# Ten transposes of r on TensorE instead of a DMA, w2 laid out by row block, score tails on ScalarE alone: an attention, MLP and soft-MoE chain on one core

## The chip, the cores and the metric

The kernel runs on one core of one Trainium2 chip. The metric is the device time of one execution in microseconds (us); the median of three runs is quoted. Engines are named as in the profile: PE (TensorE), DVE (VectorE), ACT (ScalarE), POOL (GpSimd) and SP, which here only issues DMAs. Instructions of one engine run in the order in which they stand, and wait for each other across engines by semaphores.

## The reference

Three layers follow each other. Attention has 4 batches, 8 heads, 576 positions and head size 64, with a threshold on the scores (only scores within `tau` of the row's maximum keep their weight). An MLP with a leaky ReLU follows, 512 to 2048 to 512. Last comes a soft mixture of 8 experts with 4 slots each, F = 1024.

```python
scores = scale * q @ k.T
thresh = max(scores, -1) - tau
scores = where(scores >= thresh, scores, -1e9)
attn = softmax(scores);  x = attn @ v            # x: 2304 x 512
h = x @ w_in;  g = maximum(0.01 * h, h);  x = g @ w_out
logits = x @ phi                                 # 2304 x 32
d = softmax(logits, axis=0);  slot_in = d.T @ x  # 32 x 512
for e in range(8):
    slot_out[e] = maximum(slot_in[e] @ w1[e], 0) @ w2[e]
out = softmax(logits, axis=1) @ slot_out
```

`w_in` and `w_out` come as 64-bit numbers and are turned into 32-bit ones on the chip by integer operations. `w1` and `w2` are 32-bit, 16.8 MB each.

## The kernel before

**Start (to about 135 us).** All 16 pieces of `w_in` (128 rows by 512 columns) are read as integer pairs into buffers `r`, converted by ACT, DVE and sometimes POOL (`one_chunk`, lines 606 to 680, by one of three recipes called modes 0, 1, 2; `MI` names the recipe of each of four rows), and split into a high and a low f16 part (`wh`, 8 buffers). The same is done to `w_out` (`MO`); its 32-bit form is also stored to a scratch tensor `scr`, and folded with `phi` into `wq`. The first attention tiles run beside this.

**Attention.** There are 18 tiles of 128 rows, each with four head pairs. `ends` computes the scores of the last 64 keys for all eight heads and keeps them in SBUF as `T` and their maxima in `tn`. For a head pair, `heads` computes 2 x 512 scores into PSUM (`S`, two buffers, line 1089), DVE reduces their maxima (line 1098) and forms the threshold `th` (line 1103). ACT writes the thresholded main part from `S` (two instructions of 128x512, line 1112). The tail, 2 x 64 scores, is made in two steps: POOL or DVE adds the threshold to `T` (line 1121), then ACT applies its Prelu to the sum (line 1130). An exponential follows on ACT (line 1201), then a high and low f16 split, a DMA transpose (line 1235, `aT`), and the product with `v` into `X` (line 1259).

**Feed.** For a finished tile `xT`, four chunks of 512 columns go through 12 matmuls each (line 1340, into PSUM `h` or `eT`), ACT's leaky ReLU (`g`, line 1352) and an f16 split `r` (lines 1359 to 1366). `r` is used twice: untransposed by the slot sums `M` (line 1534), and transposed, as `rT`, by the logits `L` (lines 1385 and 1389). Each of the 72 chunks is transposed by one DMA (line 1375), issued by SP. After every second tile, `block` rescales the running sums.

**Experts, after the last tile.** From the slot sums a chain of small steps leads through `w_out` (line 1650, from `scr`) to the slot inputs. They meet `w1` (line 1702) and `w2` (line 1776). `w1` and `w2` are read in 512 KB pieces into any free buffer of the tags `wh`, `qk`, `r`, `ae`, `ah`, `e2`, some halves of `w1` (256 KB, `HF` of them in pairs) into smaller tags. A buffer is free when attention or the feed no longer uses it: `qk` after the last scores, `wh` after the last feed matmuls, `r` after the last slot sum. `w2` is read as three column parts (256, 128 and 128 columns). For one part a group of matmuls needs the pieces of four experts; after a part its columns are combined, multiplied with the routing weights and written out (line 1829).

**What sets the order.** A planner in the program (`Plan.schedule`) goes through all operations with an estimated cost and a priority each, simulates the engines, and fixes both the order on every engine and the buffer that each operation gets. The table `O` holds the priorities and sizes. A new number or cost there moves many instructions. The lines of the functions that the change touches:

## Time and profile before

| | |
|---|---|
| median of 3 runs | 621.42 us (618.77 to 626.65) |
| profiled execution, its time | 618.97 us |
| span of that execution, first to last instruction | 616.8 us |
| granted TensorE clock, mean | 0.930 of full speed |
| PE busy | 541.8 us, 88% |
| DVE busy | 425.1 us, 69% |
| ACT busy | 399.5 us, 65% |
| POOL busy | 257.5 us, 42% |

Busy shares are means over the three stages, which are limited by different things. They have to be read by stretches of time. Busy time counts an instruction from its start to its end, and on ACT and DVE the next one may start before that end, so the distance of two starts is the better measure of what one instruction takes from its engine.

### The profile page before, as it was taken

What the parts mean: (1) busy time and instruction counts of PE and PEld (TensorE: products, weight loads), DVE (VectorE), ACT (ScalarE), POOL (GpSimd) and SP (SyncE); (2) the same over time, 40 slices, a digit from 0 to 9 for tenths busy, and PEclk for the clock granted to TensorE, in tenths of its full rate; (3) what the DMA queues carried; (4) which work ended last, traced back from release to release, by engine and by line L of the source; (5) the groups of instructions that cost most, each with busy time, mean ns of one, the idle gap of its engine ahead of it and who ended that gap; (6) DMA issues with size and microseconds to landing.
All of it is one profiled execution on the core that took longest, in us unless ns stands there. A gap on an engine that the chain in (4) does not pass through costs nothing.

```text
span 616.8 us, 14389 instructions
## 1 busy us (share of the span) xinstructions
PE 541.8 (88%) x5576; PEld 313.0 (51%) x5576; DVE 425.1 (69%) x930; ACT 399.5 (65%) x720; POOL 257.5 (42%) x302
## 2 busy tenths in 40 slices
PE   4787787688999999999979999999999979589884
PEld 2465575454555555555445555556555555333463
DVE  3879989996879859688787788778776555320031
ACT  3977787585777878778957877786787823221031
POOL 0243264514346545555544667573666630120000
PEclk9999667799999999999979999999999989868997
DMA  8997676654999979999989889999999999999998
GB/s 314 398 249 196 233 192 209 159 150 92 208 216 203 177 137 176 163 253 168 200 138 164 163 157 196 224 166 201 150 167 205 141 204 241 261 415 368 413 414 332
DMA packets 254388, 135.93 MB, mean 220 GB/s; under 512 B 231152, under 2 KB 231664, under 8 KB 254320
## 3 DMA queue, kind: packets, MB, share of 16 engines
q1 hardware_dynamic: 248416, 118.85, 83.6%
q10 hardware_dynamic: 5904, 16.16, 8.8%
q8 instruction: 44, 0.72, 0.5%
q14 instruction: 24, 0.20, 0.1%
HBM read 69.44 MB, written 8.91 MB: 127 GB/s over the span
## 4 chain that ended last, share of the span: by engine, by line
PE 57%; DMA 15%; DVE 13%; ACT 9%; issue 3%; POOL 1%; SPq 1%; ACTq 0%; DVEq 0%; POOLq 0%
PE h L1340 14%; PE eT L1340 10%; PE S L1089 8%; PE X L1259 7%; DMA aT<-ah 5%; PE S L1702 2%; PE S L1057 2%; PE misc L1534 2%; DMA scr<-w 2%; PE misc L858 2%; ACT ae L1112 2%; DMA qk<-in_w2q 2%; DVE nm L1098 2%; DMA wh<-in_w 2%; DMA r<-in_w2q 2%
## 5 line engine op out<-in xcount | busy, mean ns | idle before, releaser
L1222 POOL TENSOR_TENSOR ah<-ae,ah 128x512 f16<-128x512 f32 (+1 forms) x192 | 185.7, 995 | 135.8 <-DVE ah L1211 55.4
L1340 PEld LDWEIGHTS <-xT 128*128 128x128 f16 x864 | 77.8, 98 | 87.7 <-issue 12.9
L1340 PE MATMUL h<-wh,xT 128*128 128x512 f16 x492 | 120.1, 383 | 0.5 <-ACT w L848 0.2
L1112 ACT ACTIVATE ae<-S,th 128x512 f32<-128x512 f32 x144 | 93.3, 684 | 26.2 <-DVE th L1103 12.1
L1098 DVE TENSOR_REDUCE nm<-S 128x2 f32<-128x1024 f32 x72 | 86.8, 1216 | 23.1 <-PE S L1089 22.6
L1259 PEld LDWEIGHTS <-aT 128*128 128x128 f16 (+1 forms) x2016 | 75.3, 103 | 44.0 <-issue 26.1
L1089 PE MATMUL S<-qk 64*128 64x512 f32 (+1 forms) x320 | 88.1, 688 | 9.2 <-DMA qk<-in_qk 5.6
L1340 PE MATMUL eT<-wh,xT 128*128 128x512 f16 x372 | 89.7, 379 | 0.0
L1259 PE MATMUL X<-vx,aT 128*128 128x65 f16 (+1 forms) x1792 | 74.1, 199 | 9.8 <-DVE x L1295 6.2
L1201 ACT ACTIVATE ae<-ae,c 128x1152 f32<-128x1152 f32 x64 | 80.3, 1255 | 1.3
L1366 DVE TENSOR_TENSOR r<-g,r 128x512 f16<-128x512 f32 x56 | 45.2, 807 | 3.3 <-ACT r L1361 2.9
L1352 ACT ACTIVATE g<-h,c 128x512 f32<-128x512 f32 x41 | 27.9, 681 | 22.0 <-PE h L1340 20.3
L1211 DVE CAST ah<-ae 128x1152 f16<-128x1152 f32 x52 | 40.3, 775 | 2.5 <-DMA aT<-ah 1.4
L1089 PEld LDWEIGHTS S<-qk 64*128 64x128 f32 (+1 forms) x320 | 23.2, 188 | 33.1 <-ACT ae L1112 9.9
L1359 DVE CAST r<-g 128x512 f16<-128x512 f32 x37 | 20.6, 555 | 23.6 <-ACT g L1352 21.8
L858 PE MATMUL misc<-c,w 128*128 128x32 f32 x128 | 24.7, 348 | 13.7 <-ACT w L848 8.3
L1366 POOL TENSOR_TENSOR r<-g,r 128x512 f16<-128x512 f32 x16 | 20.1, 1260 | 37.5 <-DVE r L1359 27.3
L1352 ACT ACTIVATE g<-eT,c 128x512 f32<-128x512 f32 x31 | 21.1, 681 | 19.6 <-PE eT L1340 16.7
L858 PEld LDWEIGHTS misc<-c,w 128*128 128x128 f32 x128 | 22.8, 267 | 19.3 <-ACT w L848 12.2
L663 POOL TENSOR_TENSOR w<-w,qk 128x512 int32<-128x512 int32 x8 | 11.5, 1434 | 40.3 <-DVE w L646 21.5
L1103 DVE SCALAR_TENSOR_TENSOR th<-nm,c,tn 128x2 f32<-128x2 f32 x72 | 26.2, 372 | 0.5
L1057 PE MATMUL S<-qk 64*128 64x64 f32 (+1 forms) x320 | 22.7, 289 | 1.9 <-DMA qk<-in_qk 0.9
(287 smaller groups left out, 924.2 us busy)
## 6 DMA issues: line engine op xcount, KB each, us to landing
r<-in_w_in SPq DMA_DIRECT2D x16, 512.0 KB, 4.5
qk<-in_w_out SPq DMA_DIRECT2D x14, 512.0 KB, 4.9
wh<-in_w SPq DMA_DIRECT2D x11, 512.0 KB, 7.6
qk<-in_qk SPq DMA_DIRECT2D x9, 576.0 KB, 4.2
qk<-in_w SPq DMA_DIRECT2D x10, 512.0 KB, 7.4
qk<-in_qk ACTq DMA_DIRECT2D x7, 576.0 KB, 5.5
scr<-w SPq DMA_DIRECT2D x14, 256.0 KB, 3.5
vr<-in_v ACTq DMA_DIRECT2D x10, 330.0 KB, 3.9
```

The lines of the kernel that those rows point to most:

```text
L858: pe.matmul(out=wpp.ap, lhsT=wt.ap[:, k], rhs=phi.ap[:, k], start=(k == 0), stop=(k == 3))
L1057: pe.matmul(out=Tp.ap[r0:r1, i, pr * KT : pr * KT + KT], lhsT=qk[b, pr].ap[h, 0, o : o + r1 - r0], rhs=qk[b, pr].ap[h, 1, KW:S], start=(pr ...
L1089: pe.matmul(out=ps.ap[r0:r1, i], lhsT=qk[b, pr].ap[h, 0, o : o + r1 - r0], rhs=qk[b, pr].ap[h, 1, 0:KW], start=True, stop=True, skip_group ...
L1098: lambda: dve.tensor_reduce(out=nm.ap, in_=ps.ap, axis=AX.X, op=ALU.max, negate=True),
L1112: (lambda i: lambda: act.activation(out=main()[:, i], in_=ps.ap[:, i], func=AF.Prelu, bias=th.ap[:, i : i + 1], scale=1.0, alpha=2.0**90))(i),
L1201: lambda: act.activation(out=ae.ap, in_=ae.ap, func=AF.Exp, bias=nt.ap[:, 0:1], scale=0.125),
L1211: ("dve", P2(t_dve2(2 * S)), lambda: dve.tensor_copy(out=ah.ap[:, :, :S], in_=ae.ap)),
L1222: lambda: pool.tensor_tensor(out=ah.ap[:, h, w0 : w0 + c1 - c0], in0=ae.ap[:, h, c0:c1], in1=ah.ap[:, h, c0:c1], op=ALU.subtract),
L1259: pe.matmul(out=xa(2 * pr + i)[r0:r1], lhsT=w()[:, r0:r1], rhs=vtiles[b, pr].ap[:, wv, cv, 0 : D + 1], start=(n == 0 and 2 * pr + i in (0, ...
L1340: pe.matmul(out=hp.ap, lhsT=xT.ap[:, wx * 4 + k], rhs=wh(k, j, ww), start=(n == 0), stop=(n == 11),)
L1352: (lambda g, hp, j: lambda: act.activation(out=g.ap, in_=hp.ap, func=AF.Prelu, alpha=0.01, scale=hsc.ap[:, j : j + 1]))(g, hp, j),
L1366: fg = lambda eng, j, g: lambda: eng.tensor_tensor(out=r[j](1), in0=g.ap, in1=r[j](0), op=ALU.subtract)
```

## The change

**r on TensorE.** For chunks 62 to 71 of 72 (`RT=62`; the last two of tile 15 and all of tiles 16 and 17) the DMA transpose is gone. PE transposes the 32-bit `g` in four blocks into a PSUM bank that belonged to `S`, ACT copies the high part into `rT`, and DVE subtracts to get the low part. These banks can be used only after the last scores.

**w2 by row block.** A 512 KB piece of `w2` now holds the same row block for four experts, so each piece is followed by its own 8 matmuls. Before, a group of matmuls waited for four pieces. The bytes and the size of a piece stay.

**Score tails.** The addition of the threshold by POOL or DVE is gone. ACT makes the tail from `T` in two instructions of 128x64 with the threshold as bias.

**Table.** `MI` is (0, 1, 1, 1) where it was (2, 0, 0, 1): 12 of 16 pieces of `w_in` go by recipe 1 and none by recipe 2. `HF` is 8, not 9 (pairs of half pieces of `w1`); `E` has one buffer, not two; buffers named `w` are not taken by others until `w_in` is converted. Some costs and priorities differ, so the planner draws the order anew.

```diff
-        NP=1, HB=1, HF=9, LH=2.09, ... E=2, ... MI=(2, 0, 0, 1), ... TE=0.12, ... NA=23, ... PJ=0,
+        NP=1, HB=1, RT=62, TB=1, HF=8, LH=2.27, ... E=1, ... MI=(0, 1, 1, 1), ... TE=0.21, ... NA=22, ... PJ=0.02,
...
+    pl.main["w"] = ("w", "w_in")
...
         tail = lambda: two(ae.ap[:, 2 * KW :]) if flat else ae.ap[:, :, KW:S]
+        if O["TB"]:
+            for i in range(2):
+                act_op(
+                    prio - 0.01, 230,
+                    (lambda i: lambda: act.activation(
+                        out=tail()[:, i], in_=Ts.ap[:, 2 * pr + i], func=AF.Prelu, bias=th.ap[:, i : i + 1],
+                        scale=1.0, alpha=2.0**90))(i),
+                    r=[Ts, th], w=[(ae, 2 + i)],
+                )
+            return
...
+            if 4 * t + j >= O["RT"]:
+                tp = bank([P, 4, P])
+
+                def f(g=g, tp=tp):
+                    for c in range(4):
+                        pe.transpose(tp.ap[:, c], g.ap[:, c * P : (c + 1) * P], ident.ap)
+
+                pe_op(p + 0.05, 530, f, r=[g, ident], w=[tp, rT[j]], work=427)
+                act_op(
+                    p + 0.05, t_act(512), (lambda j, tp: lambda: act.activation(
+                        out=rT[j].ap[:, 0:4], in_=tp.ap, func=AF.Copy))(j, tp), r=[tp], w=[(rT[j], 0)],
+                )
+                dve_op(
+                    p + 0.05, 608, (lambda j, tp: lambda: dve.tensor_tensor(
+                        out=rT[j].ap[:, 4:8], in0=tp.ap, in1=rT[j].ap[:, 0:4], op=ALU.subtract))(j, tp),
+                    r=[tp, (rT[j], 0), wq], w=[(rT[j], 1)],
+                )
+                continue
             dma_t(
...
-            if hf:
-                groups = [[load(a["w2q"][hf - 1, 4 * G + j], T0 - 7 + 0.1 * hf, [P, 8, QC]) for j in range(4)]]
-            else:
-                groups = [
-                    [load(a["w2"][4 * G + j, n], T0 - 7, [P, 4, HC]) for j in range(4)] for n in range(2)
-                ]
+            m = wd // QC
+            for x in range(4 * m):
+                w = load(
+                    a["w2q"][hf - 1, G, x] if hf else a["w2"][G, x], T0 - 7 + 0.1 * hf, [P, 4, 1024 // wd // 4, wd]
+                )
+                nc_ = 2 // m
...
-                    r=[(hts[G], (j, m)) for j in range(4) for m in ([n] if hf == 0 else [0, 1])] + ws
+                    r=[(hts[G], (j, nc_ * x // 4)) for j in range(4)] + [w]
```

The order moves at three places that matter below. Line numbers in the new order are those of the changed file, some 3 to 41 higher.

The first is SP's queue from the last transposes of attention (`aT`) and of r (`rT`) to the first pieces of `w1` (`in_w`) that go into `wh`, the feed's weight buffers. Before:

```order
L1375 DMA_TRANSPOSE rT<-r 128x8x128 x4
L1682 DMA qk<-in_w 128x1024
L1682 DMA x_7878<-in_w 128x512
L1682 DMA qk<-in_w 128x1024
L1682 DMA ah<-in_w 128x1024
L1375 DMA_TRANSPOSE rT<-r 128x8x128 x3
L1682 DMA ah<-in_w 128x1024
L1682 DMA wh<-in_w 128x1024 x2
L1375 DMA_TRANSPOSE rT<-r 128x8x128 x4
L1682 DMA rT<-in_w 128x512
L1682 DMA wh<-in_w 128x1024 x2
```

With the change:

```order
L1249 DMA_TRANSPOSE aT<-ah 128x9x128 x4
L1416 DMA_TRANSPOSE rT<-r 128x8x128
L1714 DMA qk<-in_w 128x1024 x2
L1649 DMA vx<-scr 128x512
L1714 DMA qk<-in_w 128x1024
L1649 DMA vx<-scr 128x512
L1714 DMA ah<-in_w 128x1024 x2
L1714 DMA x_7931<-in_w 128x512
L1714 DMA wh<-in_w 128x1024 x4
L1714 DMA r<-in_w 128x1024 x2
L1714 DMA wh<-in_w 128x1024 x2
```

No transpose stands between or behind the pieces of `w1` any more, and two pieces of `scr` have come to SP.

The second is ACT at the last chunks of the feed, from the rescaling of the block before (`dh`) to the last `g`, the leaky ReLU. Before:

```order
L1352 ACTIVATE g<-h,c_1354 128x512
L1513 ACTIVATE dh<-misc,c_4566 128x64
L1352 ACTIVATE g<-eT,c_1354 128x512
L1361 ACTIVATE r<-g 128x512
L1352 ACTIVATE g<-h,c_1354 128x512
L1420 ACTIVATE c_2064,c_2065<-lg,sm 128x32
L1352 ACTIVATE g<-eT,c_1354 128x512
L1420 ACTIVATE c_2064,c_2065<-lg,sm 128x32
```

With the change (`rT<-S` is the copy of a transposed chunk out of PSUM):

```order
L1554 ACTIVATE dh<-misc,c_5282 128x64
L1405 ACTIVATE rT<-S_77 128x512
L1375 ACTIVATE g<-h,c_1335 128x512
L1461 ACTIVATE c_2129,c_2130<-lg,sm 128x32
L1405 ACTIVATE rT<-S_77 128x512
L1375 ACTIVATE g<-eT,c_1335 128x512
L1405 ACTIVATE rT<-S_76 128x512
L1375 ACTIVATE g<-h,c_1335 128x512
L1405 ACTIVATE rT<-S_76 128x512
L1461 ACTIVATE c_2129,c_2130<-lg,sm 128x32
```

A copy of a chunk has come in behind each `g`, and the last copy follows the last `g` directly.

The third is ACT at a late head pair: main part, tail, feed, exponential. Before:

```order
L1112 ACTIVATE ae<-S_77,th 128x512 x2
L1130 ACTIVATE ae<-ae 128x2x64
L1201 ACTIVATE ae<-ae,c_116 128x1152
L1361 ACTIVATE r<-g 128x512 x2
L1352 ACTIVATE g<-h,c_1354 128x512
```

With the change:

```order
L1116 ACTIVATE ae<-S_77,th 128x512 x2
L1126 ACTIVATE ae<-T,th 128x64 x2
L1375 ACTIVATE g<-h,c_1335 128x512
L1215 ACTIVATE ae<-ae,c_116 128x1152
L1322 ACTIVATE xT<-h 128x512
```

Two instructions make the tail where one finished it, and they read `T` and `th` instead of a sum made elsewhere.

## Rows read from the trace of the kernel before

**Rows 1.** The page's slices: busy tenths in 40 equal slices of the span.
```profile
PE   4787787688999999999979999999999979589884
```

**Rows 2.** Two stretches: busy per engine (count), granted clock, DMA share, GB/s.
```profile
45.00:135.00 90.00, 68.42 (x517) 49.20 (x517) 85.70 (x190) 66.64 (x131) 37.91 (x34) 0.75 0.67 190
180.00:480.00 300.00, 293.83 (x3329) 162.24 (x3328) 235.72 (x484) 230.74 (x394) 174.73 (x196) 0.99 0.99 179
```

**Rows 3.** Groups by line and form, w_in's conversion: count, busy us, mean ns, idle before.
```profile
L638 DVE TENSOR_SCALAR w<-rT 128x512 int32<-128x512 int32 x17 | 9.0, 546 | 3.0 <-DMA scr<-w 2.7 <-ACT rT L611 0.2
...
L670 DVE SCALAR_TENSOR_TENSOR w<-rT,w 128x512 int32<-128x512 int32 x11 | 8.0, 726 | 0.0
...
L663 POOL TENSOR_TENSOR w<-w,r 128x512 int32<-128x512 int32 x4 | 5.5, 1370 | 11.9 <-DVE w L646 11.9
...
L622 ACT ACTIVATE r<-r,c 128x512 int32<-128x512 uint32 x4 | 3.1, 784 | 1.8 <-DMA r<-in_w_in 1.8
```

**Rows 4.** Groups by line and form, the score tails: count, busy us, mean ns.
```profile
L1130 ACT ACTIVATE ae<-ae 128x128 f32<-128x128 f32 x72 | 22.4, 311 | 1.9 <-DVE ae L1121 1.7
...
L1121 DVE TENSOR_TENSOR ae<-T,th 128x128 f32<-128x128 f32 x52 | 19.0, 366 | 4.1 <-POOL ah L1222 3.3 <-ACT T L1067 0.5
```

**Rows 5.** ACT in order of time: start us, us, instruction, idle before and its releaser.
```profile
483.88 0.31 ACT L1130 ACTIVATE ae<-ae 128x128 f32<-128x128 f32 x1
484.08 0.69 ACT L1352 ACTIVATE g<-h,c 128x512 f32<-128x512 f32 x1
...
485.83 0.32 ACT L1420 ACTIVATE c<-lg,sm 128x32 f32<-128x32 f32 x1
486.06 0.18 ACT L1420 ACTIVATION_READ_ACCUMULATOR c<-lg,sm 128x1 f32 x1
...
513.00 0.60 ACT L1308 ACTIVATE xT<-h 128x512 f16<-128x512 f32 x1 [0.98 <-PE h L1304]
```

**Rows 6.** PE in order of time, end of attention and of the feed.
```profile
496.35 0.93 PE L1259 MATMUL X<-vx,aT 128*128 128x65 f16 x14 [2.95 <-DVE x L1295]
...
512.36 0.60 PE L1304 MATMUL h<-c,x 128*128 128x128 f32 x4
512.80 1.46 PE L1340 MATMUL eT<-wh,xT 128*128 128x512 f16 x6
...
527.14 1.46 PE L1340 MATMUL eT<-wh,xT 128*128 128x512 f16 x6
...
535.30 0.23 PE L1385 MATMUL misc<-c,rT 128*128 128x64 f16 x1 [0.66 <-DMA rT<-r]
```

**Rows 7.** DVE in order of time: the split of a transposed tile.
```profile
513.63 0.69 DVE L1313 TENSOR_TENSOR xT<-h,xT 128x512 f16<-128x512 f32 x1 [0.42 <-ACT xT L1308]
```

**Rows 8.** SP's queue in order of time.
```profile
525.09 8.65 SPq L1375 DMA_TRANSPOSE rT<-r  x4
...
561.20 1.98 SPq L1682 DMA_DIRECT2D qk<-in_w  x3
```

**Rows 9.** Stretches of the end, columns as in Rows 2.
```profile
530.00:535.00 5.00, 1.26 (x24) 0.93 (x24) 0.57 (x1) 0.00 (x0) 0.00 (x0) 0.86 1.09 216
...
575.00:580.00 5.00, 5.00 (x84) 3.09 (x80) 0.84 (x8) 0.62 (x2) 0.00 (x0) 1.00 1.03 410
...
610.00:617.00 7.00, 0.89 (x5) 0.48 (x3) 1.29 (x2) 1.47 (x3) 0.00 (x0) 0.65 0.58 224
```

**Rows 10.** Chain that ended last, in order of time: start us, us, what.
```profile
526.84 8.41 DMA rT<-r x2
...
540.10 2.68 PE misc L1534 x24
...
557.67 10.36 PE S L1702 x80
...
593.55 11.10 DMA qk<-in_w2q
...
604.69 3.14 PE X L1776 x58
```

More of the change, by code (lines that the diff above doesn't have):

```diff
@@ L200, in place @@
             for tg in b.tag:
-                st = self.main.get(tg, tg)
-                if b.stream != st and b.stream not in self.early and pos.get(st, 0) < len(self.order.get(st, ())):
+                st = self.main.get(tg, (tg,))
+                if b.stream not in st and b.stream not in self.early and any(
+                    pos.get(x, 0) < len(self.order.get(x, ())) for x in st
+                ):
                     n, after = self.quota.get((b.stream, tg), (0, 0))
-                    if held[b.stream, tg] >= n or pos[st] < after:
+                    if held[b.stream, tg] >= n or pos[st[0]] < after:
                         continue
@@ L1062, in ends @@
         pe_op(
-            prio, 550, f, r=[qk[b, pr] for b in tile_parts(t) for pr in range(4)],
+            prio, 1040, f, r=[qk[b, pr] for b in tile_parts(t) for pr in range(4)],
             w=[Tp, tn, Ts], work=427,
@@ L1146, in f @@
                     pe.transpose(tp.ap[:, c - c0], ae.ap[:, c * P : (c + 1) * P], ident.ap)
-            pe_op(p2, 135 * n, f, r=[(ae, key), ident], w=[tp, (eT, key)], work=107 * n)
+            pe_op(p2, 135 * n, f, r=[(ae, k) for k in ((key,) if key < 2 else (2, 3))] + [ident], w=[tp, (eT, key)], work=107 * n)
             act_op(
@@ L1324, in emit, with bank @@
     HG = O["HG"]
+    banked = []
+    def bank(shape):
+        uniq[0] += 1
+        n = f"bk{uniq[0]}"
+        pl.early.add(n)
+        b = pl.buf(("B0", "B1", "B2", "B3"), shape, F32, n)
+        banked.append(b)
+        return b
     def feed(t, xT):
@@ L1598, in hbuf @@
         return pl.buf(("h", "eT"), shape, F32, f"hb{uniq[0]}")
-    def bank(shape):
-        uniq[0] += 1
-        n = f"bk{uniq[0]}"
-        pl.early.add(n)
-        b = pl.buf(("B0", "B1", "B2", "B3"), shape, F32, n)
-        banked.append(b)
-        return b
-    banked = []
     WO = T0 - 8
@@ L1862, in host @@
     w2 = np.asarray(inputs["moe2_w2"]).reshape(8, 2, P, 4, 4, P)
-    wa = w2[:, :, :, :, :2].reshape(8, 2, P, 4, 256)
-    wz = w2[:, :, :, :, 2:].transpose(4, 0, 2, 1, 3, 5).reshape(2, 8, P, 8, P)
+    w2 = w2.reshape(2, 4, 2, P, 4, 512).transpose(0, 2, 4, 3, 1, 5).reshape(2, 8, P, 4, 512)
+    wa = w2[..., :256]
+    wz = w2[..., 256:].reshape(2, 4, 2, P, 4, 2, P).transpose(5, 0, 1, 3, 4, 2, 6)
     def bits(w):
```

50 lines of the change are left out of this document (25 added, 25 removed).

## The prediction

> **What bounds the kernel now.** I read the slices of the page first [rows 1], then stretches of time, then the chain that ended last and the engines' own lists. Three stages show. Up to about 135 us PE is not full, because the converted weights are late: from 45 to 135 us DVE is busy 85.70 of 90 us, ACT 66.64 and PE 68.42, at a granted clock of 0.75 [rows 2]. From 180 to 480 us PE is the bound: 293.83 of 300 us at clock 0.99, with ACT at 230.74 and DVE at 235.72 [rows 2]. There at most 6.2 us can be had by any better order. The third stage is the end. The last feed matmuls start at 527.14 and end near 528.4, but the last logits start only at 535.30, released by the transposing DMA of r [rows 6]; the chain of waits books 8.41 us to that DMA [rows 10]. SP needs 8.65 us to issue the last four transposes [rows 8], and the reads of the expert weights stand behind them in that queue. Then a chain of small steps leads to `w1` at 557.67, and afterwards the reads set the pace: 410 GB/s with PE busy too [rows 9], while the chain books 11.10 us to the last awaited piece of `w2`, then 3.14 us to the matmuls behind it [rows 10]. What the change is worth is decided at the two ends, not in the middle.
>
> The profiled execution took 618.97 us (span 616.8, 2.2 around it). The median of the runs is 621.42, that is 2.45 above. The terms are summed against 618.97, and 2.45 is added for the median. I take 2% as what a measurement of this kernel can tell from no change: the three runs are spread over 1.3%.
>
> **Start.** By the two orders, up to the last write of the feed weights DVE loses 8 shifts (0.55 each by the mean) and gains 5 two-input integer steps (0.73 each), so 4.4 against 3.7 us [rows 3], and loses 8 tail additions of 0.37, 2.9 us [rows 4]. DVE gets 3.6 us less. POOL loses the four integer additions of 1.37 us on pieces of `w_in` [rows 3]. ACT has 8 more low-part steps in place of 4 cheaper ones, at most 8 x 0.78 = 6.3 us [rows 3], and dearer tails, below; its slack of 23 us in this stretch covers that if it falls well. DVE being 95% busy, I take 2.5 us of the 3.6 as time. Bounds: -5, if the POOL steps removed had also stretched DVE, and +2, if ACT becomes the late one. One buffer fewer for `E`, the guard on buffers `w`, and the shifted priorities I cost at nothing: the block steps have a whole tile pair between them. If that cover fails, a wait of one block step, below half a microsecond, comes up in each of 9 blocks; it lies within the bounds.
>
> **Score tails.** One ACT step of 128 columns takes 0.20 us from start to start (483.88 to 484.08), and one of 32 columns with a bias takes 0.23 (485.83 to 486.06) [rows 5]. Two tails of 64 columns with a bias are therefore between 0.40 and 0.52 us; I take 0.46. That is 0.26 more per head pair, 18.7 us of ACT over 72 pairs [rows 4]. In the middle stage some 15 us of it come on top of 230.74, ACT goes to 82%, and PE stays the bound [rows 2]. The cover is ACT's idle time; the exponential behind the tail is the one that is late if it fails. In return DVE loses 52 additions of 0.37 us [rows 4] and POOL the other 20, neither of them a bound there. Time: 0, with bounds -3 (half of PE's 6.2 us of idle time closes) and +18.7 (all of it shows).
>
> **r on TensorE.** The nearest rows are those of a tile `x`, which goes the same way. Four transposes take 0.44 us of PE (512.36 to the next matmul at 512.80) [rows 6], ACT's copy starts 0.64 after them and DVE's split 0.63 after that, ending at 514.32 [rows 5, 7]. From PE's start to a finished transposed chunk it is 1.96 us. PE thus gets 10 x 0.44 = 4.4 us of new work in a stretch that it fills; ACT gets 6 us and DVE 7, both half idle there. Against this, the last logits wait for about 0.8 us of leaky ReLU and 1.96 us, so they come 2.8 us after the last feed matmuls and not 6.9 us: -4.1. PE's wait of 2.95 us at 496.35 [rows 6] stood in the old order; I count half of it closed, -1.5, between nothing and all. The slot sums, which started 4.8 us behind the last logits (540.10) [rows 10], then come 7.6 us after the last feed matmuls and not 11.7. From 530 to 535 us the clock was still 0.86 [rows 9]; at the lower level the sums took 2.68 us [rows 10], at the higher one they would take half. I count half of that gain, -0.6. Together 4.4 - 4.1 - 1.5 - 0.6 = -1.8 us for the start of `w1`, with bounds +0.5 and -6.5 (the whole wait closed, and the clock held through `w_out` too).
>
> **The reads.** From 530 to 535 us the DMA engines moved 216 GB/s, 1.08 MB, which is nearly the four transposes of 0.262 MB alone [rows 9]: 1.25 us each, where plain reads at 410 GB/s need 0.64. Without them, and with the reads no longer behind them on SP, the `wh` pieces start as their buffers come free; about 7 us of reading come earlier. But the buffers are finite: the first `w2` pieces were issued at 561.20, 3.5 us after `w1` had started to give buffers back [rows 8, 10]. From there 30 pieces at 1.28 us are 38.4 us, and the last landed at 604.65, 43.45 us later; the other 5 us were backlog and a lower rate. With the change the gate opens 1.8 us earlier, 31 pieces are left and not 30 (+1.3, one pair of halves of `w1` fewer), and I count 3.5 us of the 5 us of backlog as gone, since the queue has caught up. Sum: -4.0 us for the last piece. Bounds: 0 (the gate decides and moves little) and -9 (the reads alone decide).
>
> [...]
>
> **The last step.** The last awaited group of 64 matmuls took 3.14 us after the last read [rows 10]; with eight per piece it is 0.4, so 2.7 less. After the reads the writes still move 224 GB/s of a possible 410 [rows 9], so part of the tail is transfer; I take -2, between 0 and -2.7. The pieces' size and the sum of their bytes do not move, so that layout itself costs nothing in reading.
>
> **Sum.** -2.5 + 0 - 4.0 - 2 = -8.5 us: 610.5 for an execution like the profiled one, **613** as the median, 1.4% below 621.42. Its own range, with the bounds of the single terms not all on one side, is 606 to 619.
>
> **Rivals.**
>
> First, the reads gain little: `w1` starts as late as before because PE's 4.4 us of transposes eat what the missing wait gives, and the pieces of `w2` wait for buffers as they did. For it speaks that PE fills the slices up to there [rows 1], so that its new work finds no hole; against it the 6.9 us of waiting before the logits. Only the start and the last step are left: -4.5, so 617. Chance 0.18.
>
> Second, all of it comes: start -4, the gate -6.5 with the clock held, the reads nearly -9, the last step -2.5, which gives about 603. For it speaks that the reads already run at 410 GB/s wherever they have buffers. Chance 0.20.
>
> Third, slower: ACT's two tails are the price. Every head pair needs ACT to clear `S` before PE may write the next scores. If ACT, at 82% or more and in order, comes late by its extra 0.26 us at each of 72 pairs, +18.7 us come on PE's path, less the gains of the end: 618.97 + 18.7 - 6.0 + 2.45 makes 634; with two thirds of it 628. It decides from the point where ACT's step in a pair, tails included, takes longer than PE's work per pair. Against it speaks that ACT has 69 idle us in 300. Chance 0.11 for 624 and more. [...]
>
> The forecast keeps 0.51. The **range 602 to 622** leaves out most of the third rival and the lower end of the second. Faster by over 2% means below 609.0: the second rival and about a quarter of the forecast, 0.32. Slower by over 2% means above 633.8: half of the third, 0.05. The rest is 0.63.
>
> **What would show it.** In the new profile no transpose of r stands on SP after the last one of attention. The last logits start within 3.5 us of the last feed matmuls. `w1` starts 14 to 18 us after that, and some 2 us earlier in the span than 557.67, apart from the shift of the start. The reads show no stretch of 216 GB/s near the end of the feed, and a short dip where the buffers are full. The matmuls behind the last piece of `w2` take under 1 us. PE is busy over 290 us between 180 and 480. If PE waits there for `ae`, the third rival is right; if the DMA rate falls well below 400 GB/s for over 6 us before the first pieces of `w2`, the gate decides and the first rival is right. The forecast is wrong if the feed begins later in the span than before, since everything behind it shifts.

## The result and the profile after

The changed kernel takes **604.86 us** (median of 4 runs, 602.83 to 617.41) against 620.96 for the kernel before in the same series. The ratio is 0.972, with a 95% interval of 0.967 to 0.978: 2.8% faster. One slow run of each kernel, 617.41 and 626.65 us, is left out of the ratio (the medians of the others, 603.44 and 620.51, lie 17.1 us apart), and the profiles of e1, e5 and e11 below are of slow runs too, so only waits within a stretch are read from them. The forecast was 613, 8.4 us below its median of 621.42; the gain is twice that, and the time lies near the lower end of the range. The profiled execution took 602.83 us, with a span of 601.0.

Where the 15.8 us between the two profiled executions lie is seen when the span is cut at four places on TensorE: the end of the last feed matmuls, the first slot-sum matmul of the last block, the first of `w1`, and the end. The right column is what the forecast's terms give for the stretch. Single differences can be 0.1 off by rounding.

| stretch, us | before | after | difference | forecast |
|---|---|---|---|---|
| up to the last feed matmuls | 528.6 | 520.8 | -7.8 | +0.4 (-2.5 + 0 + 4.4 - 1.5) |
| from there to the slot sums | 11.4 | 7.6 | -3.9 | -4.1 |
| from there to `w1` | 17.6 | 14.2 | -3.4 | -0.6 |
| from there to the end | 59.1 | 58.4 | -0.7 | -4.2 (-2.2 - 2) |

**The first stretch.** These are windows of the trace after: busy time of each engine with its count, then TensorE's granted clock, the DMA share and GB/s. The first two answer to [rows 2], the other three cut TensorE's full stage in parts.

```profile
45.00:135.00 90.00, 69.81 (x554) 48.83 (x553) 85.13 (x186) 74.93 (x148) 30.62 (x29) 0.75 0.70 203
180.00:480.00 300.00, 297.21 (x3424) 162.97 (x3422) 225.96 (x461) 244.22 (x454) 168.78 (x187) 1.00 1.02 181
...
215.00:330.00 115.00, 112.94 (x1228) 61.42 (x1225) 85.33 (x172) 95.65 (x179) 63.02 (x70) 1.00 1.03 182
330.00:480.00 150.00, 149.46 (x1762) 81.89 (x1758) 112.94 (x232) 117.84 (x220) 86.91 (x97) 1.00 1.02 180
480.00:520.83 40.83, 40.73 (x436) 24.46 (x428) 28.02 (x57) 20.22 (x39) 11.44 (x12) 1.00 0.96 244
```

The same three parts in the trace before, the last one up to its own last feed matmuls:

```profile
215.00:330.00 115.00, 110.43 (x1194) 61.60 (x1193) 89.82 (x204) 87.84 (x153) 62.01 (x70) 0.97 0.98 176
330.00:480.00 150.00, 148.44 (x1715) 80.99 (x1712) 114.61 (x223) 115.01 (x194) 88.58 (x98) 1.00 0.98 180
480.00:528.60 48.60, 44.17 (x491) 25.13 (x489) 25.22 (x58) 21.73 (x44) 15.37 (x16) 0.96 1.04 203
```

TensorE's idle time is the window less its busy time: 4.57 + 1.56 + 4.43 = 10.6 us before, 2.06 + 0.54 + 0.10 = 2.7 after. The clock adds to it: 0.97 over 110 busy us and 0.96 over 44 cost 3.3 + 1.8 = 5.1 us before and nothing after. Together that is 13.0 us less, minus the 4.4 us of new transposes (ten of 0.44, the distance from 518.93 to 519.37 below): -8.6, which is the whole of the first line of the table and 0.8 more. So nothing is left for the start: the first feed matmul does come earlier (110.68, not 114.92), but the 17th of the 144 leaky ReLUs on scores starts at 112.41 and started at 113.03.

**The wait for r.** TensorE in order of time in the trace after (start, duration, instruction, idle before it and its releaser):

```profile
518.93 0.60 PE L1401 MATMUL S<-c,g 128*128 128x128 f32 x4
519.37 1.46 PE L1363 MATMUL h<-wh,xT 128*128 128x512 f16 x6
521.67 0.66 PE L1401 MATMUL S<-c,g 128*128 128x128 f32 x4 [0.84 <-ACT g L1375]
523.74 0.19 PE L1430 MATMUL misc<-c,rT 128*128 128x32 f16 x1 [0.52 <-DVE rT L1409]
...
528.38 2.59 PE L1575 MATMUL misc<-r,dh 128*32 128x512 f16 x24
...
536.50 0.62 PE L1682 MATMUL eT<-raw,g 128*32 128x512 f32 x2 [0.75 <-ACT g L1674]
...
542.62 0.62 PE L1734 MATMUL S<-e,xT 128*32 128x512 f32 x1 [0.45 <-DVE xT L1702]
```

The last feed matmuls end at 520.8, the last logits start at 523.7, 2.9 us later where 2.8 was said and 6.9 stood before [rows 6]. One matmul of `w_out` takes 0.59 to 0.62 us here, at a clock of 1.00 (536.5 to 539.5 us); before it took 1.06 at 0.50 (549.2 to 552.7).

**The tails.** ScalarE in order of time, to be set beside [rows 5]:

```profile
479.02 0.60 ACT L1126 ACTIVATE ae<-T,th 128x64 f32<-128x64 f32 x2
479.50 0.70 ACT L1375 ACTIVATE g<-eT,c 128x512 f32<-128x512 f32 x1
```

Two tails take 0.48 us from start to the next start; 0.46 was the estimate from rows.

**The reads and the end.** Windows of the trace after, then SP's waits (total us, times, longest), then the end of the chain of waits (start, us, what), then the matmuls that wait for the last piece of `w2`:

```profile
535.00:540.00 5.00, 4.16 (x36) 1.36 (x36) 0.37 (x2) 0.60 (x1) 0.00 (x0) 1.00 0.61 220
...
555.00:560.00 5.00, 5.00 (x64) 2.28 (x58) 0.36 (x4) 1.09 (x2) 0.00 (x0) 1.00 1.03 410
```

```profile
SPq L1714 <- PE eT L1682: 6.4, 3, 5.7
...
SPq L1714 <- PE misc L1575: 5.1, 2, 4.7
```

```profile
542.62 8.79 PE S L1734 x80
552.43 4.24 PE S L1734 x37
556.67 10.53 DMA wh<-in_w
567.26 10.00 DMA r<-in_w2q
577.32 10.04 DMA qk<-in_w2q
587.43 6.51 DMA out<-wh
```

```profile
588.67 1.08 PE L1807 MATMUL X<-ah,ae 128*32 128x128 f32 x16 [0.62 <-DMA ah<-in_w2q]
```

Without the transposes the reads still fall to 220 GB/s for a while, because SP now waits for buffers that `w_out` and the slot sums give back. From 545 us on the DMA engines run without a pause, first with reads, then with writes, until 597: at 375 GB/s to 550 and at 409 to 421 from there. The chain ends in a write, no longer in the matmuls behind the last piece [rows 10].

### The profile page after: what moved, and what is told of

It reads as the page before. It is cut to its first block, busy times and chain, and to the rows that moved or that the text cites. A ratio compares the mean times of both kernels' runs of the same rounds, so it can differ in the third digit from the quotient of the medians.

```text
span 601.0 us, 14465 instructions
## 1 busy us (share of the span) xinstructions
PE 532.2 (89%) x5616; PEld 305.0 (51%) x5616; DVE 413.9 (69%) x890; ACT 417.3 (69%) x796; POOL 243.5 (41%) x282
## 4 chain that ended last, share of the span: by engine, by line
PE 32%; DMA 9%; issue 5%; DVE 5%; ACT 4%; POOL 2%; ACTq 0%; SPq 0%; DVEq 0%; POOLq 0%
PE h L1363 7%; PE eT L1363 7%; PE S L1093 5%; PE X L1273 4%; DMA aT<-ah 2%; PE S L1734 2%; DMA wh<-in_w 2%; DMA qk<-in_w2q 2%; DMA r<-in_w2q 2%; PE misc L1575 1%; ACT ae L1116 1%; POOL ah L1236 1%; PE S L1061 1%; DVE nm L1102 1%; DMA out<-wh 1%
## 5 line engine op out<-in xcount | busy, mean ns | idle before, releaser
L1363 PEld LDWEIGHTS <-xT 128*128 128x128 f16 x864 | 78.0, 98 | 88.9 <-issue 14.1
L1363 PE MATMUL h<-wh,xT 128*128 128x512 f16 x492 | 118.1, 379 | 1.4 <-ACT w L852 1.0
L1273 PEld LDWEIGHTS <-aT 128*128 128x128 f16 (+1 forms) x2016 | 73.3, 102 | 33.4 <-issue 22.8
L1273 PE MATMUL X<-vx,aT 128*128 128x65 f16 (+1 forms) x1792 | 71.7, 196 | 0.8 <-DMA aT<-ah 0.8
L1225 DVE CAST ah<-ae 128x1152 f16<-128x1152 f32 x53 | 42.1, 794 | 11.3 <-DMA aT<-ah 7.5
L1382 DVE CAST r<-g 128x512 f16<-128x512 f32 x47 | 25.7, 553 | 32.2 <-ACT g L1375 29.4
L1126 ACT ACTIVATE ae<-T,th 128x64 f32<-128x64 f32 x144 | 43.1, 351 | 0.0
L1093 PEld LDWEIGHTS S<-qk 64*128 64x128 f32 (+1 forms) x320 | 23.1, 188 | 36.9 <-ACT ae L1116 12.5
L1389 DVE TENSOR_TENSOR r<-g,r 128x512 f16<-128x512 f32 x51 | 37.6, 741 | 6.1 <-ACT r L1384 5.5
L1389 POOL TENSOR_TENSOR r<-g,r 128x512 f16<-128x512 f32 x21 | 24.9, 1190 | 39.5 <-DVE r L1382 32.7
L1375 ACT ACTIVATE g<-h,c 128x512 f32<-128x512 f32 x41 | 28.1, 685 | 16.0 <-PE h L1363 14.2
L1375 ACT ACTIVATE g<-eT,c 128x512 f32<-128x512 f32 x31 | 21.2, 683 | 18.8 <-PE eT L1363 16.1
L1107 DVE SCALAR_TENSOR_TENSOR th<-nm,c,tn 128x2 f32<-128x2 f32 x72 | 28.7, 406 | 0.3
L862 PE MATMUL misc<-c,w 128*128 128x32 f32 x128 | 21.8, 321 | 7.4 <-ACT w L852 4.4
L862 PEld LDWEIGHTS misc<-c,w 128*128 128x128 f32 x128 | 20.6, 243 | 13.6 <-ACT w L852 6.6
```

Of the source, the lines that this page charges most:

```text
L862: pe.matmul(out=wpp.ap, lhsT=wt.ap[:, k], rhs=phi.ap[:, k], start=(k == 0), stop=(k == 3))
L1093: pe.matmul(out=ps.ap[r0:r1, i], lhsT=qk[b, pr].ap[h, 0, o : o + r1 - r0], rhs=qk[b, pr].ap[h, 1, 0:KW], start=True, stop=True, skip_group ...
L1126: (lambda i: lambda: act.activation(out=tail()[:, i], in_=Ts.ap[:, 2 * pr + i], func=AF.Prelu, bias=th.ap[:, i : i + 1], scale=1.0, alpha= ...
L1225: ("dve", P2(t_dve2(2 * S)), lambda: dve.tensor_copy(out=ah.ap[:, :, :S], in_=ae.ap)),
L1273: pe.matmul(out=xa(2 * pr + i)[r0:r1], lhsT=w()[:, r0:r1], rhs=vtiles[b, pr].ap[:, wv, cv, 0 : D + 1], start=(n == 0 and 2 * pr + i in (0, ...
L1363: pe.matmul(out=hp.ap, lhsT=xT.ap[:, wx * 4 + k], rhs=wh(k, j, ww), start=(n == 0), stop=(n == 11),)
```

## The experiments

In e1 to e4, e8 and e11 to e15 the order on every engine stays the same as in the kernel that was edited, but for the instructions that the edit itself adds or takes away and a few steps of the last stage; in e9 and e10 it stays the same altogether. In e5 to e7 it is drawn anew by the same numbers. All ratios are to the kernel before, in the same series, with 95% intervals. These are the four stretches of the table above in the profiled executions of all runs but e5 and e6:

| us | last feed | to slot sums | to w1 | to the end |
|---|---|---|---|---|
| before / after | 528.6 / 520.8 | 11.4 / 7.6 | 17.6 / 14.2 | 59.1 / 58.4 |
| e1, e3 | 541.5, 537.5 | 7.4, 12.3 | 17.7, 13.1 | 57.9, 59.9 |
| e9, e13, e14 | 534.5, 531.3, 537.3 | 11.3, 10.2, 7.6 | 14.3, 14.4, 14.3 | 60.9, 60.5, 58.9 |
| e2, e4 | 524.0, 518.6 | 13.1, 8.0 | 17.5, 13.1 | 57.9, 59.8 |
| e7, e8, e10 | 527.0, 524.4, 535.6 | 7.5, 7.4, 7.4 | 17.7, 15.8, 16.2 | 58.2, 59.6, 58.5 |
| e11, e12, e15 | 529.7, 520.6, 525.2 | 8.6, 10.8, 7.5 | 14.1, 17.8, 14.4 | 59.1, 57.4, 53.7 |

**e1: r on TensorE alone, in the kernel before.**

```diff
+        RT=62,                                # in the table of numbers
+            if 4 * t + j >= O["RT"]:
+                tp = bank([P, 4, P])
...
+                continue
             dma_t(
```

> The kernel before, with the one change that the last ten chunks of r are turned by TensorE; the order stays as it was apart from these ten steps. Theory A (r is most of it: its transposes cost nothing, because they fall into holes of TensorE that the transposing DMAs had made, and the shorter wait lets the clock recover): the last feed matmuls end no more than 1 us later in the span than 528.4, no hole of TensorE over 1.5 us is left between 485 us and that end, the slot sums start 7.7 us behind them and not 11.7, w1 starts 15 us after the last feed matmuls and not 29, and the time falls by 6 to 10 us (611 to 615). Theory B (the order drawn anew closed the holes; r's own part is as forecast): the last feed matmuls end 3 to 4 us later, the hole of 2.95 us stays or halves, w1 starts 1 to 2 us earlier than 557.67, and the time falls by 1 to 4 us.

Measured: 620.02 us, ratio 0.9958 (0.9924 to 0.9992), about 2.6 us less. The window from 480 us to the last feed matmuls, to be set beside 480.00:528.60 above:

```profile
480.00:541.52 61.52, 57.11 (x592) 33.29 (x588) 38.97 (x81) 32.52 (x63) 18.35 (x20) 0.97 0.88 204
```

TensorE is still idle for 4.41 us there, as in the kernel before (4.43), and the hole before X is still 2.96 us long (at 505.30). The transposes close no hole; they come on top, as the forecast's +4.4 had it. Theory B holds: in the old order r is worth little.

**e2: the changed kernel with r by DMA.**

```diff
-        NP=1, HB=1, RT=62, TB=1, ...
+        NP=1, HB=1, RT=72, TB=1, ...
```

> The changed kernel with all of r turned by DMA again and the rest of the change kept. Theory A: holes of TensorE of 1 us and more come back before the last feed matmuls, which do not end earlier than 520.65 although 4.4 us of transposes are gone; the slot sums start 11 to 12 us behind them, w1 6 to 8 us later than 542.62 from the first feed matmul on, and the time rises by 6 to 10 us, to 611 to 615. Theory B: the last feed matmuls end 4 us earlier, the slot sums start as late as in the changed kernel, and the time rises by 0 to 3 us.

Measured: 611.22 us, 0.9824 (0.9766 to 0.9883). So 10.9 us are gained without r, and r in the new order gives the other 6.3 (the two intervals leave 1 to 11). From 480 us to the last feed matmuls:

```profile
480.00:524.02 44.02, 41.88 (x435) 22.26 (x434) 25.44 (x51) 21.11 (x41) 14.54 (x15) 1.00 1.09 198
```

TensorE is idle for 2.14 us here, in three waits of 0.7, against 4.43 in the old order and 0.10 in the changed kernel. Most of the holes are closed by the new order and a part by r. The slot sums start 13.1 us behind the last feed matmuls, a little later than both theories had it for the DMA. The rise of 6.3 us is that of theory A, but not for its reason: theory B is right that the order does most.

**e3 and e4: the clock held by idle matmuls**, in the kernel before and in the changed one.

```diff
+    def warm(k):
+        for _ in range(WARM.get(k, 0)):
+            pe.matmul(
+                out=junk_b[0].ap, lhsT=wq.ap[:, 0:2].rearrange("p a b -> p (a b)"),
+                rhs=wq.ap[:, 0:8].rearrange("p a b -> p (a b)"), start=True, stop=True,
+            )
```

> The kernel before, with 36 matmuls of 512 columns on constants, whose result nobody reads, in the pauses of TensorE between the last feed matmuls and the last weight product ahead of w1. Nothing else is moved. Theory of the clock (what the shorter pause gave back is the clock): the granted clock stays at 1.00 from 528 to 555 us, w_out takes 3.8 us and not 6.09, the slot sums 1.4 and not 2.7, w1 starts 3 to 5 us earlier than 557.67, and the time falls by 2 to 4 us. Rival (the small steps wait for ScalarE and VectorE, the reads set the end): w1 starts at most 1 us earlier and the time moves by less than 1 us.

> The changed kernel, with 20 such matmuls in the same pauses. Theory of the clock: between 524 and 530 us the clock stays at 1.00 and not 0.50, the slot sums take 1.4 us and not 2.6, w1 starts 1.5 to 2.5 us earlier than 542.62 and the reads, which wait there for buffers, follow: 1 to 2 us less, near 603. Rival: the reads are the bound behind that point whatever opens them, the time moves by less than 0.7 us.

Measured: e3 622.84 us, 1.0035 (0.9996 to 1.0073); e4 605.41 us, 0.9742 (0.9682 to 0.9801). The stage between the last feed and `w1`, in the kernel before and in e3:

```profile
528.00:558.00 30.00, 18.38 (x129) 8.50 (x131) 7.67 (x22) 7.08 (x17) 5.09 (x15) 0.71 1.03 354
```

```profile
536.00:564.00 28.00, 23.17 (x183) 10.81 (x183) 8.27 (x24) 7.01 (x17) 5.10 (x15) 0.94 1.07 348
```

The clock was held, 0.94 and not 0.71, and `w1` starts 25.3 us behind the last feed matmuls instead of 29.1. The time did not follow in either kernel. In e4 `w1` starts 0.6 us earlier behind the last feed matmuls (21.2 and 21.8), and the stretch from `w1` to the end is 1.4 us longer, which takes that back. In e3 no gain in the median was seen at all; it may be that most executions of the kernel before have the higher clock there anyway, which one profile can't tell. The table shows something more: the stretch from the slot sums to `w1` takes 14.1 to 14.4 or 15.8 to 17.8 us in kernels of both kinds, 14.3 and 14.4 in e9 and e13 with the long wait for r, 17.7 in e7 with the short one. The rows of e9 and e7 differ in the clock, 0.91 and 0.70, and in TensorE's busy time with it:

```profile
545.73:560.06 14.33, 10.11 (x84) 4.48 (x83) 4.02 (x7) 4.43 (x8) 2.91 (x10) 0.91 1.03 415
```

```profile
534.58:552.25 17.67, 13.44 (x84) 5.61 (x83) 4.02 (x7) 4.48 (x8) 2.89 (x9) 0.70 0.72 253
```

So the length of the wait does not decide the clock there. That it differs between executions of one kernel is likely, since the mean clock of the kernel before lies between 0.895 and 0.942 over its runs of 616 to 625 us, but each kernel was profiled only once.

**e5: the order drawn anew, alone. e6: the tails back. e7: the kinds of integer steps back.**

```diff
-        NP=1, HB=1, RT=62, TB=1, ...
+        NP=1, HB=1, RT=72, TB=0, ...          # e5, with w2's old layout and loop too
+        NP=1, HB=1, RT=62, TB=0, ...          # e6
-        ... MI=(0, 1, 1, 1),
+        ... MI=(2, 0, 0, 1),                  # e7
```

> The order drawn anew with its other kinds of integer steps and one buffer fewer for E, but r turned by DMA, the tails of scores as before (an addition on VectorE or GpSimd, then ScalarE) and w2 laid out as before. Theory O (the order is most of what the middle gained): the hole of 3.3 us before X at 309 to 313 us and the clock of 0.66 behind it are gone, TensorE is busy over 98 us of 280 to 380, the first feed matmul comes at 111 us and not 115, and the time is 611 to 614. Theory T (the tails on ScalarE are what made room on VectorE): without them holes behind VectorE of 3 us and more stay somewhere in 180 to 480, the feed starts at 113 to 115, and the time is 617 to 621.

> The changed kernel with the tails of scores by an addition on VectorE or GpSimd and one step of ScalarE, as before, the order drawn for it by the same numbers. Theory O: within 2 us of the changed kernel, 603 to 607. Theory T: 4 to 8 us slower, 609 to 613, with the feed starting 2 to 4 us later than 110.7 and a hole behind VectorE. By the forecast's third rival the tails cost time, then this one is faster: below 602.

> The changed kernel with the kinds of integer steps (the shifts and low parts of the packed weights) as before, GpSimd's four pieces among them, the order drawn for it by the same numbers. If the start's gain is theirs: the first feed matmul comes at 114 to 115 us and not at 110.7, and the time rises by 3 to 5 us, to 608 to 610. If the tails or the order made it: the feed starts within 1 us of 110.7 and the time moves by less than 2 us.

Measured: e5 636.67 us, 1.021 (1.016 to 1.027); e6 637.76 us, 1.026 (1.021 to 1.031); e7 614.02 us, 0.989 (0.985 to 0.993). Each is far outside what was expected. The window of 180 to 480 us in e6:

```profile
180.00:480.00 300.00, 284.83 (x3263) 156.28 (x3261) 221.08 (x476) 218.54 (x379) 162.45 (x182) 0.98 0.96 177
```

TensorE is idle for 15.2 us in it, and in the same window of e5 for 22.6 and of e7 for 8.7, against 2.8 in the changed kernel. The numbers that set the order fit the work of the changed kernel better than any of these three; with one kind of work changed they draw a worse order, in e5 and e6 one that is worse than the old. These three runs don't tell what the tails or the steps cost by themselves, since the order went with them.

**e8: w2 laid out as before**, in the changed kernel.

```diff
-            m = wd // QC
-            for x in range(4 * m):
+            if hf:
+                groups = [[load(a["w2q"][hf - 1, 4 * G + j], T0 - 7 + 0.1 * hf, [P, 8, QC]) for j in range(4)]]
...
```

> The changed kernel with w2 laid out and multiplied as before, everything else in the same order. By the forecast's terms (last step -2, reads): the last 64 matmuls take 3.1 us again, the span from w1's start to the end grows by 2 to 3 us, the time rises by 2 to 3 us, to 607 to 608. Rival (from w1 on the transfers are the bound, reads and writes together, and the writes fill the time in which TensorE is late): the last matmuls are later, the span from w1's start to the end stays within 1 us of 58.4, and the time within 1 us.

Measured: 606.82 us, 0.9744 (0.9690 to 0.9798); the changed kernel stands at 0.972. From `w1` to the end it is 59.6 us against 58.4, with the last group of matmuls ending the chain again:

```profile
591.44 5.48 PE X L1808 x128
```

About 1 us of the layout arrives, within what these intervals leave open. The 4.2 us that the forecast gave the last stage are not there.

**e9: the tails on ScalarE in the old order. e10: the tails undone in the new order.**

```diff
-                (n, c, (lambda eng: lambda: eng.tensor_tensor(... op=ALU.add))(eng))
+                (n, c, lambda: None)          # e9: nothing on VectorE or GpSimd,
...                                            # two ACTIVATEs with bias in the place of one
+            add = pool if (4 * t + pr) % 18 >= 13 else dve
+            for i, fn in enumerate((          # e10: the addition, then one ACTIVATE
```

> The kernel before, its order on every engine unchanged, with the additions of the tails gone from VectorE and GpSimd and two steps of ScalarE with a threshold as bias in the place of the one. Theory T (the tails make room on VectorE whatever the order): the feed starts 1 to 3 us before 114.9, the hole of 3.3 us before X at 309 to 313 us shrinks or goes, and the time falls by 3 to 8 us, to 613 to 618. Theory J (tails and order count only together: the numbers that set the order were chosen with the tails on ScalarE): the hole stays, the time moves by less than 2 us either way. By the forecast's third rival it rises by 10 us and more.

> The changed kernel, its order unchanged, with the additions back on VectorE (52) and GpSimd (20) at the place of the first of the two ScalarE steps, and one ScalarE step behind them. Theory T: TensorE waits for ScalarE's tails and for VectorE, the time rises by 4 to 8 us, to 609 to 613. Theory J: the order has room for both, the time moves by less than 2 us, and the 33 us that the redrawn order without the tails lost were that order's, not the tails'. By the forecast's third rival it falls.

Measured: e9 624.76 us, 1.0029 (0.9990 to 1.0068); e10 617.42 us, 0.9931 (0.9891 to 0.9970). In the old order 52 additions less on VectorE give nothing, and 72 dearer tails on ScalarE cost nothing that could be measured; the hole of 3.3 us stays. In the new order, taking the tails out costs 12.5 us, more than theory T had. The windows of e10:

```profile
215.00:330.00 115.00, 107.15 (x1118) 57.22 (x1115) 82.74 (x173) 83.47 (x144) 59.54 (x68) 0.97 0.98 169
330.00:480.00 150.00, 144.73 (x1703) 80.12 (x1701) 116.54 (x242) 109.07 (x184) 88.14 (x98) 1.00 0.99 173
```

7.85 and 5.27 us of idle time are back, where the changed kernel has 2.06 and 0.54: 3.8 us of it is one wait for a DMA transpose of `ah`, and 4.7 us are six waits for ScalarE's step that clears `S`. Theory J holds for the old order only: the order and the tails are worth something together. The additions of e10 stand where the planner left no place for them, so the 12.5 us are what the tails are worth in this order, and not what they would be worth against an order drawn well for additions; no run has one with the rest of the change.

**e11 and e12: fewer chunks of r on TensorE**, four and two, not ten.

```diff
-        NP=1, HB=1, RT=62, TB=1, ...
+        NP=1, HB=1, RT=68, TB=1, ...          # e11
+        NP=1, HB=1, RT=70, TB=1, ...          # e12
```

> The changed kernel with four chunks of r (the last tile's) turned by TensorE and not ten; the order is otherwise the same. If the transposes cost TensorE their full time where it has no holes (the difference of e2): the last feed matmuls end 6 x 0.44 = 2.6 us earlier, the wait behind them stays as short, and the time falls by 2 to 3 us, to 602 to 603. Rival: six transposes of 0.262 MB come back to SP's queue and to the DMA engines; logits of the tile before wait for them in TensorE's order, the last feed matmuls end no earlier, and the time is the same or up to 3 us longer.

> The changed kernel with only the last two chunks of r turned by TensorE. By the same reasoning the last feed matmuls end 3.5 us earlier; the first two chunks of the last tile by DMA are there in time if they land within 4 us of their split, then the slot sums start 7.5 us behind the last feed matmuls and the time falls by 3 to 4 us. Rival: those two transposes are late, the slot sums start 9 us and more behind the last feed matmuls, and the time is that of four chunks or longer.

Measured: e11 608.56 us, 0.9759 (0.9686 to 0.9832); e12 609.07 us, 0.9759 (0.9673 to 0.9846). Neither is faster than the changed kernel. With two chunks the slot sums start 10.8 us behind the last feed matmuls, as the rival said: TensorE waits for the transposes by DMA.

```profile
525.10 0.23 PE L1426 MATMUL misc<-c,rT 128*128 128x64 f16 x1 [2.73 <-DMA rT<-r]
```

With four the wait stays short (8.6 us), and the 2.6 us expected from TensorE were not seen; the intervals would not show them with certainty, and the profiles do not settle it: that of e11 ends the feed 8.9 us later, with a wait near 180 us that is 4.3 us longer (told at the end).

**e13 and e14: one hole out of the old order**, without and with r on TensorE.

```diff
+        z = max(at["z", EARLY, 0], at["z", EARLY, 1])
+        mine = [at["rz", EARLY], at["x", EARLY, 0], at["x", EARLY, 1]]
+        return seq[: z + 1] + [seq[i] for i in mine] + [s for i, s in enumerate(seq) if i > z and i not in mine]
```

The hole in the trace before, on TensorE, then VectorE's steps that TensorE waited for, then the stretch behind it:

```profile
312.63 0.93 PE L1259 MATMUL X<-vx,aT 128*128 128x65 f16 x14 [3.26 <-DVE x L1295]
```

```profile
309.12 0.15 DVE L1284 TENSOR_SCALAR z<-misc 128x1 f32<-128x1 f32 x1
309.18 1.57 DVE L1366 TENSOR_TENSOR r<-g,r 128x512 f16<-128x512 f32 x1
310.68 0.19 DVE L1289 RECIPROCAL rz<-z 128x8 f32<-128x8 f32 x1
310.79 1.17 DVE L1098 TENSOR_REDUCE nm<-S 128x2 f32<-128x1024 f32 x1
311.88 0.61 DVE L1295 TENSOR_TENSOR x<-X,rz 128x448 f32<-128x448 f32 x1
```

```profile
313.00:319.00 6.00, 6.00 (x51) 3.80 (x50) 4.89 (x21) 3.81 (x6) 2.37 (x3) 0.54 0.70 121
```

VectorE did two things first that TensorE was not waiting for (a subtraction of r and a maximum over the next scores). The pause cost its 3.26 us and then, at a clock of 0.54 over 6 us, 2.8 us more.

> The kernel before; on VectorE alone, in one tile, the three steps that turn X into x stand ahead of one subtraction of r and one maximum over S (0.78 and 1.1 us), behind which they stood. If the hole is a part of what the new order gained: the hole of 3.26 us at 309 to 313 us shrinks to 1.3 or less (-1.9), the clock stays at 1.00 behind it (-2.9, half of the 5.9 us at 0.50), and the time falls by 3 to 5 us, to 617 to 619. Rival: what is late next takes its place (the maximum, 0.8 us later, holds the next thresholds), the clock falls all the same, and the time falls by less than 2 us.

> The kernel of e13 with the last ten chunks of r turned by TensorE as in e1. If the gains add: 3 to 5 us below e1, 0.983 to 0.991 of the kernel before, 611 to 616. Rival: as e1, 0.996.

Measured: e13 619.46 us, 0.9952 (0.9919 to 0.9985), 3.0 us less; e14 617.42 us, 0.9950 (0.9919 to 0.9982). TensorE's waits of 308 to 320 us in e13, and the six us that answer to the window above:

```profile
PE X L1270 <- DVE x L1307: 0.9, 1, 0.9
PE h L1353 <- DVE c L576: 0.9, 1, 0.9
PE misc L1547 <- ACT ae L1123: 0.8, 1, 0.8
PE h L1353 <- DVE xT L1326: 0.7, 1, 0.7
```

```profile
313.00:319.00 6.00, 3.44 (x52) 2.36 (x53) 5.94 (x18) 3.87 (x7) 2.22 (x4) 1.00 1.06 140
```

One wait of 3.3 us has become four of under 1 us, together as long, but the clock no longer falls. What was gained is the clock's part, 3.0 us by the runs (0.9 to 5.1 by the interval) and 2.8 by the rows. With r beside it, 5.6 us were expected and 3.1 measured; its interval (1.1 to 5.0) does not show that the two add, nor rule it out, since the two parts have intervals as wide.

**e15: fewer reads.**

```diff
+                if not hf or x % 2 == 0:
                     w = load(
                         a["w2q"][hf - 1, G, x] if hf else a["w2"][G, x], ...
```

> The changed kernel without reading 8 of the 16 pieces of w2's last two quarters (the matmuls use the piece read before it; all else stays). If the transfers are the bound from w1 on: 8 x 1.28 = 10.2 us less from the start of w1 to the end, 48 to 50 and not 58.4, and a time of 594 to 596. Rival (the chain behind the last matmuls and the start of w1 set the end): 2 to 4 us less.

Measured: 601.84 us, 0.9659 (0.9608 to 0.9710). From `w1` to the end it is 53.7 us and not 58.4, so 4.7 of the 10.2 us arrive.

```profile
575.00:580.00 5.00, 5.00 (x86) 4.01 (x89) 0.42 (x1) 0.38 (x1) 0.00 (x0) 0.52 1.02 416
580.00:585.00 5.00, 4.53 (x122) 3.38 (x112) 0.69 (x1) 0.87 (x2) 0.00 (x0) 1.00 0.30 120
```

When the reads are over, at 580 us, the DMA engines fall to 120 GB/s and TensorE is the one that is full. Both theories have a part: the transfers are the bound of the last stage, and TensorE's matmuls and the writes behind them are less than 5 us behind.

No kernel that does the whole work beats the changed one by more than its interval.

## Why the prediction was wrong

**The step that failed is the first stretch: +0.4 us up to the last feed matmuls, where -7.8 was measured.** The terms that were wrong are the order and the tails: the prediction wrote of "the shifted priorities" that "I cost at nothing", and put the score tails at "Time: 0". It had two reasons: that from 180 to 480 us "at most 6.2 us can be had by any better order", and that what the change is worth is decided "at the two ends, not in the middle". The window was read as one piece: 293.83 busy us of 300 at a clock of 0.99 [rows 2] looked full. Its idle time was not spread out. It had one hole of 3.26 us, and the clock of 0.99 was 0.54 for six us and 1.00 for the rest. The stretch behind 480 us, with 4.43 us of idle time at 0.96, stood outside the window, and of it only the hole at 496.35 [rows 6] was counted, by half. The three parts together had 10.6 us of idle time and 5.1 us of lost clock to give; the forecast took 1.5 of them. The bound of 6.2 us was not broken, since idle time from 180 to 480 us fell by 3.4; but nothing of it was counted, and the clock was left out.

What closed them is the new order together with the tails on ScalarE. e2 has all of that without r and stands 10.9 us below the kernel before, part of it from w2's layout. The tails alone give nothing (e9), an order drawn by the same numbers without them is up to 16 us above the kernel before (e5, e6), and the new order loses 12.5 us when the additions come back (e10). So the term of 0 for the tails was right in the old order and wrong in the new one, and the third rival, that ScalarE's tails are the price, is refuted in the old order, where e9 lies within 0.7% of the kernel before, and in the new one, where taking the tails away makes the kernel slower. e13 shows one hole's part, 3.0 us. Which choices of the order close the others is not settled by these runs; the single buffer for `E`, `HF` and the guard on buffers `w` were tried by no run of their own.

**Start.** -2.5 was said. The feed starts 4.2 us earlier, but the windows from 215 us on account for all of the first stretch, so nothing of it is left there. e7 does not tell what GpSimd's four steps cost, since its order was drawn anew.

**r on TensorE.** The mechanism and the sizes held: 4.4 us of transposes come on top (in e1 the idle time stays at 4.41 us), the last logits start 2.9 us behind the feed, and the slot sums come 7.4 to 7.6 us behind it in seven of the eight profiles of the table with ten chunks on TensorE (8.0 in e4 with its idle matmuls), against 10.2 to 13.1 by DMA. In the new order r is worth more by the medians, 6.3 us and not 2.6. By the profiles of e2 and the changed kernel this has two parts: the wait of the DMA is longer there (13.1, not 11.4), and 2.0 us of holes ahead of the last feed matmuls go with it. Neither was foreseen.

**The clock.** -0.6 was said and -3.4 stands in the two profiles. But e9 and e13, with the long wait, have the same 14.3 and 14.4 us as the changed kernel, and e7 and e12 have 17.7 and 17.8. So no run shows it as a term of the change; that the two profiled executions fell on different sides is as far as is known chance. In the rows it is the clock, 0.69 before and 0.92 after:

```profile
540.03:557.67 17.64, 13.48 (x84) 5.62 (x83) 4.03 (x7) 4.50 (x8) 2.90 (x9) 0.69 1.03 414
```

```profile
528.38:542.62 14.24, 9.97 (x84) 4.49 (x83) 4.03 (x7) 4.43 (x8) 2.89 (x9) 0.92 0.76 255
```

Held by force (e3, e4) it moved `w1` and not the time.

**Reads and last step.** -4.2 was said behind the start of `w1`, and -0.7 was measured in the profiles, about -1 by e8. Of the reads' 2.2 us, 1.0 came: the matmuls that wait for the last piece start 46.0 us after `w1`'s start (588.67) where it was 47.0. The last step did happen: those matmuls take 1.08 us, not 3.14. (The 0.4 us of the forecast set eight matmuls of the program against 64 of the trace, where those eight are 16; that makes it 0.8.) But the forecast took the chain behind the last read as the end, while the DMA engines had the writes still to do. At 410 GB/s without a pause they fill the time that the matmuls gave back. The forecast's own remark that part of the tail is transfer was the right one, and should have made the term close to zero. The sign "no stretch of 216 GB/s" failed too: the reads fall to 220 where they wait for buffers. The rate is 255 GB/s over the 14 us ahead of `w1`, which was the sign for the first rival: the reads did gain little, as it said, though not its time of 617.

The errors did not cancel: the forecast had 8.2 us too little gain in the first stretch and 2.8 too little ahead of `w1`, and 3.5 too much behind it. The range of 602 to 622 holds the measured time by luck: its lower end was made of gains at the gate, the reads and the last step. The second rival, 603 us, had the right time for the same wrong reasons, and its terms do not add up to it: with the gate inside the reads' 9 us they give 606, with the gate beside them 599. Two more signs failed. One transpose of r does stand behind the last of attention on SP, at 495.81. And `w1` started 15 us earlier in the span, not some 2; its 14 to 18 us hold from the slot sums (14.2) and not from the last logits (18.9).

## What to carry to other kernels

A mean over a long window hides what an order can still give: cut a full stage into parts, list the waits of over 2 us of the engine that is the bound, and read the granted clock behind each, since a pause can be paid for twice (here 3.26 us of waiting and 2.8 us of clock). Where a table of numbers draws the order, its numbers belong to the exact work they were chosen for; the order and the work are to be priced together, and an experiment on one of them has to hold the order fixed. Behind the last read, ask first what the writes still need: a shorter chain gives little while they fill the DMA engines (here 0.7 us of the 4.2 forecast, at 410 GB/s).

## What the runs showed of the hardware

**A short pause can be paid for twice, and not always.** After 3.26 us without a matmul the clock was 0.54 from 313 to 319 us, though TensorE was full again from 312.63; four pauses of under 1 us in the same stretch left it at 1.00 (e13). Behind the same pause, over the 6 us from its end, it was 0.51 in the kernel before, 0.54 in e3, and 0.72 in e9. In e8 a pause of 2.66 us at 176.23 cost no clock at all, where the changed kernel shows 0.72 behind 2.59 us of the same wait:

```profile
176.23:182.23 6.00, 5.28 (x73) 3.40 (x74) 5.69 (x10) 1.99 (x3) 2.55 (x3) 1.00 0.50 192
```

```profile
173.38:179.38 6.00, 5.28 (x53) 2.79 (x54) 5.27 (x9) 1.31 (x2) 2.55 (x3) 0.72 0.52 192
```

**One group of transposing DMAs takes longer in one execution than in another.** Up to 180 us, e2 runs the same instructions in the same order on every engine as the changed kernel. In the changed kernel two transposes `aT<-ah` held SP for 6.52 us at 160.34, and in e2 for 8.60. VectorE may not write `ah` before they have read it (it stands idle for 4.87 us until 172.56 in the changed kernel), and TensorE waits for VectorE. The same instruction in the changed kernel and in e2:

```profile
173.38 0.30 PE L1198 MATMUL misc<-vx,ah 128*128 128x65 f16 x4 [2.59 <-DVE ah L1178]
```

```profile
179.86 0.40 PE L1198 MATMUL misc<-vx,ah 128*128 128x65 f16 x4 [9.51 <-DVE ah L1178]
```

In other profiles of this order the wait is 8.6 (e15), 6.9 (e11), 4.0 (e12), 2.7 (e8) and 0.6 us (e4), and it is the longer the longer SP was held: 8.22, 7.99, 7.40, 6.58 and 6.22 us. In e15 the chain of waits books 13.83 us to this transfer, in e8 9.39. A single profile of this kernel therefore says little of a change of a few us before 180 us, and the stretches are better compared from behind that place. What makes these transposes take longer was not tried, and how much of the spread of the times comes from here is not shown.
